# SwiGLU on one core: first loads in pairs from two queues, a block of x turned on TensorE, up of the first tiles on 512 columns

## The chip, the cores and the metric

One core of one Trainium2 chip. The metric is the device time of one execution in microseconds (us), as the median over several executions; profiles are of single executions on the same core. A profile's span is about 1.8 us shorter than the time of its execution (81.3 against 83.13 for the kernel before).

Words used below: DVE is the vector engine (VectorE); SP is the engine that issues most of the DMAs (`nc.sync`). A "gate" or an "up" is one matmul of the gate or up product; the "ups of the first tiles" are those of F tiles 0 to 3. A "D block" is 128 of the 512 values of D. A "turn" is a matmul with the identity that swaps rows and columns of a 128 x 128 piece of x; its result lies in PSUM and is copied to SBUF ("the copy"). A load has "landed" when all its bytes have arrived.

## The reference

```python
# x: (32, 32, 512); w1, w3: (512, 1792); w2: (1792, 512); all bfloat16
gate = einsum("bsd,df->bsf", x, w1)
up   = einsum("bsd,df->bsf", x, w3)
out  = einsum("bsf,fd->bsd", silu(gate) * up, w2)
```

With the first two axes of x flattened there are 1024 rows. Gate and up are computed transposed, F on partitions (14 tiles of 128) and rows along the free axis in two blocks of 512, each as 4 matmuls over the D blocks of 128.

## The kernel before

TensorE needs x with D on partitions. The first 256 rows are loaded plainly and turned on TensorE; rows 256 to 511 (the "second quarter" below) and the second block of 512 come by transposing DMAs. While the data arrive, the first four F tiles are worked on by halves of 256 columns.

```python
    nc.sync.dma_start(out=x_sb[:], in_=x_view[:, 0 : HB // P, :])            # HB = 256
    for w_sb, w_v in ((w1_sb, w1_v), (w3_sb, w3_v)):
        load_w(w_sb, w_v, 0, FK, 0, 2)       # tiles 0..3, D blocks 0 and 1; FK = 4
        load_w(w_sb, w_v, 0, FK, 2, DT)      # tiles 0..3, D blocks 2 and 3
    nc.sync.dma_start_transpose(out=xT[:, :, HB:NB], in_=x_flat[HB:NB, :])   # NB = 512
    # ... the other loads of w1 and w3, the second block of x, w2 (cut) ...

    keep_warm(6, NB)                          # matmuls of ones, to warm TensorE up
    keep_warm(2, P)
    transpose_slab(0, nc.vector.tensor_copy)  # two transposes into PSUM (bf16), one copy
    transpose_slab(1, nc.scalar.copy)
    keep_warm(3, P)
    gates = [bank("gate_ps") for _ in range(FK)]
    for dt in range(DT):                      # gates of tiles 0..3, first 256 columns
        for fo in range(FK):
            project(gates[fo], w1_sb, fo, 0, HB, [dt])
        if dt == 0:
            transpose_slab(2, nc.vector.tensor_copy)
            transpose_slab(3, nc.scalar.copy)
    ups = [bank("up_ps") for _ in range(FK)]
    for dt in range(DT):                      # ups of tiles 0..3, first 256 columns
        for fo in range(FK):
            project(ups[fo], w3_sb, fo, 0, HB, [dt])
    for fo in range(FK):                      # second 256 columns of both
        project(gates[fo], w1_sb, fo, HB, NB, range(DT), HB)
        project(ups[fo], w3_sb, fo, HB, NB, range(DT), HB)
        swiglu(gates[fo], ups[fo], fo, 0)     # ScalarE sigmoid, two DVE products
    # ... all other tiles on 512 columns, then the output matmuls (cut) ...
```

Of the kernel before, what the change touches and what calls it, by code (L numbers as in the profile page):

```python
# [9 lines left out]
@with_exitstack  # L10
def kernel(
    ctx: ExitStack,
    tc: tile.TileContext,
    x: bass.AP,
    w1: bass.AP,
    w3: bass.AP,
    w2: bass.AP,
    out: bass.AP,
):
    nc = tc.nc  # L20
    P = nc.NUM_PARTITIONS
    fp32 = mybir.dt.float32
    bf16 = mybir.dt.bfloat16
    SIGMOID = mybir.ActivationFunctionType.Sigmoid

    B, S, D = x.shape
    F = w1.shape[1]
    N = B * S
    NB = 512
    HB = NB // 2  # L30
    DT = D // P
    FT = F // P
    NT = N // P
    NBLK = N // NB
    assert D % P == 0 and F % P == 0 and N % NB == 0

    x_flat = x.flatten_outer_dims()
    out_flat = out.flatten_outer_dims()
    w1_v = w1.rearrange("(dt p) f -> p dt f", p=P)
    w3_v = w3.rearrange("(dt p) f -> p dt f", p=P)  # L40
    w2_v = w2.rearrange("(ft p) d -> p ft d", p=P)

    consts = ctx.enter_context(tc.tile_pool(name="consts", bufs=1))
    work = ctx.enter_context(tc.tile_pool(name="work", bufs=3))
    psum = ctx.enter_context(tc.tile_pool(name="psum", bufs=8, space=bass.MemoryType.PSUM))

    ctx.enter_context(tc.manual_schedule())

    x_view = x_flat.rearrange("(nt p) d -> p nt d", p=P)
    ident = consts.tile([P, P], bf16, name="ident")  # L50
    make_identity(nc, ident[:])
    x_sb = consts.tile([P, HB // P, D], bf16, name="x_sb")
    xT = consts.tile([P, DT, N], bf16, name="xT")
    w1_sb = consts.tile([P, DT, F], bf16, name="w1_sb")
    w3_sb = consts.tile([P, DT, F], bf16, name="w3_sb")
    w2_sb = consts.tile([P, FT, D], bf16, name="w2_sb")
    hT = consts.tile([P, FT, N], bf16, name="hT")

    FK = 4

    def load_w(w_sb, w_v, c0, c1, d0=0, d1=DT):
        f0, f1 = c0 * P, c1 * P
        nc.sync.dma_start(out=w_sb[:, d0:d1, f0:f1], in_=w_v[:, d0:d1, f0:f1])  # L63

    nc.sync.dma_start(out=x_sb[:], in_=x_view[:, 0 : HB // P, :])  # L65
    for w_sb, w_v in ((w1_sb, w1_v), (w3_sb, w3_v)):
        load_w(w_sb, w_v, 0, FK, 0, 2)
        load_w(w_sb, w_v, 0, FK, 2, DT)
    nc.sync.dma_start_transpose(out=xT[:, :, HB:NB], in_=x_flat[HB:NB, :])
    for c0, c1 in ((FK, 6), (6, 10), (10, FT)):  # L70
        load_w(w1_sb, w1_v, c0, c1)
        load_w(w3_sb, w3_v, c0, c1)
    nc.sync.dma_start_transpose(out=xT[:, :, NB:N], in_=x_flat[NB:N, :])
    FH = FT // 2
    nc.sync.dma_start(out=w2_sb[:, 0:FH, :], in_=w2_v[:, 0:FH, :])
    nc.sync.dma_start(out=w2_sb[:, FH:FT, :], in_=w2_v[:, FH:FT, :])

    one = nc.const_aps.tensor(1.0, [P, 1], bf16)
    table = consts.tile([P, 1], fp32, name="table")
    nc.scalar.activation(table[:], one, SIGMOID)  # L80

    def bank(name):
        return psum.tile([P, NB], fp32, name=name, tag="bank")

    warm_ps = bank("warm_ps")

    def keep_warm(n, cols):
        for _ in range(n):
            nc.tensor.matmul(  # L89
                warm_ps[:, 0:cols],  # L90
                lhsT=one.to_broadcast([P, P]),
                rhs=one.to_broadcast([P, cols]),
                start=True,
                stop=True,
            )

    def transpose_slab(dt, copy):
        pT = psum.tile([P, HB], bf16, name="pT", tag="bank")
        for nt in range(HB // P):
            nc.tensor.transpose(  # L100
                pT[:, nt * P : (nt + 1) * P], x_sb[:, nt, dt * P : (dt + 1) * P], ident[:]
            )
        copy(xT[:, dt, 0:HB], pT[:])  # L103

    def project(ps, w_sb, fo, n0, n1, dts, c0=0):
        for dt in dts:
            nc.tensor.matmul(  # L107
                ps[:, c0 : c0 + n1 - n0],
                lhsT=w_sb[:, dt, fo * P : (fo + 1) * P],
                rhs=xT[:, dt, n0:n1],  # L110
                start=(dt == 0),
                stop=(dt == DT - 1),
            )

    def swiglu(gate_ps, up_ps, fo, nb):
        sig = work.tile([P, NB], fp32, name="sig")
        nc.scalar.activation(sig[:], gate_ps[:], SIGMOID)  # L117
        t = work.tile([P, NB], fp32, name="t")
        nc.vector.tensor_mul(t[:], gate_ps[:], sig[:])  # L119
        nc.vector.tensor_mul(hT[:, fo, nb * NB : (nb + 1) * NB], t[:], up_ps[:])  # L120

    keep_warm(6, NB)
    keep_warm(2, P)
    transpose_slab(0, nc.vector.tensor_copy)
    transpose_slab(1, nc.scalar.copy)
    keep_warm(3, P)
    gates = [bank("gate_ps") for _ in range(FK)]
    for dt in range(DT):
        for fo in range(FK):
            project(gates[fo], w1_sb, fo, 0, HB, [dt])  # L130
        if dt == 0:
            transpose_slab(2, nc.vector.tensor_copy)
            transpose_slab(3, nc.scalar.copy)
    ups = [bank("up_ps") for _ in range(FK)]
    for dt in range(DT):
        for fo in range(FK):
            project(ups[fo], w3_sb, fo, 0, HB, [dt])
    for fo in range(FK):
        project(gates[fo], w1_sb, fo, HB, NB, range(DT), HB)
        project(ups[fo], w3_sb, fo, HB, NB, range(DT), HB)  # L140
        swiglu(gates[fo], ups[fo], fo, 0)

    for nb in range(NBLK):
        for fo in range(FK if nb == 0 else 0, FT):
            gate_ps = bank("gate_ps")
            project(gate_ps, w1_sb, fo, nb * NB, (nb + 1) * NB, range(DT))
            up_ps = bank("up_ps")
            project(up_ps, w3_sb, fo, nb * NB, (nb + 1) * NB, range(DT))
            swiglu(gate_ps, up_ps, fo, nb)

    for nt in range(NT):
        last = nt == NT - 1
        c0 = 0
        for DB in (D // 2, D // 4, D // 4) if last else (D,):
            o_ps = psum.tile([P, DB], fp32, name="o_ps", tag="bank")
            for fo in range(FT):
                nc.tensor.matmul(  # L157
                    o_ps[:],
                    lhsT=hT[:, fo, nt * P : (nt + 1) * P],
                    rhs=w2_sb[:, fo, c0 : c0 + DB],  # L160
                    start=(fo == 0),
                    stop=(fo == FT - 1),
                )
            o_sb = work.tile([P, DB], bf16, name="o_sb", tag="o_sb")
            if last:
                nc.vector.tensor_copy(o_sb[:], o_ps[:])  # L166
            else:
                nc.scalar.copy(o_sb[:], o_ps[:])  # L168
            nc.sync.dma_start(
                out=out_flat[nt * P : (nt + 1) * P, c0 : c0 + DB],  # L170
                in_=o_sb[:],
            )
            c0 += DB
# [30 lines left out]
```

## Time and profile before

| | kernel before |
|---|---|
| time, median of 3 (range) | 82.82 us (82.79 to 83.15) |
| span of the profile | 81.3 us |
| TensorE busy | 77.5 us, 95% |
| DVE / ScalarE busy | 48% / 28% |
| load that TensorE waits for last | w1, D blocks 2 and 3 of the first tiles: issued 1.75, landed 6.60 |
| last matmul starts | 78.40 us |

TensorE is one unbroken chain from 6.65 us to the end. The lines are in the prediction.

### The profile page before, as it was taken

Reading aid. Unit: us, or ns where it says so; the run is one execution under the profiler, and the core shown is the slowest. Engines: PE = TensorE matmul, PEld = TensorE weight load, DVE = VectorE, ACT = ScalarE, POOL = GpSimd, SP = SyncE. Lnnn points to the kernel's source line nnn. Section 1 sums busy time; section 2 is a strip of 40 time slices with the busy share of each in tenths; the row PEclk is TensorE's granted clock in tenths of the full one; section 3 lists DMA queues with packets and bytes.
Section 4 is the critical chain, followed back from the end, with each engine's and each line's share of the span. In section 5 each row is a group of like instructions: output and inputs, shape, how many; then the busy total and the mean of one; then the engine's idle time right before and its main releaser. Section 6 shows DMA issues by size and latency. Waiting matters only on the chain.

```text
span 81.3 us, 1079 instructions
## 1 busy us (share of the span) xinstructions
PE 77.5 (95%) x415; PEld 39.9 (49%) x415; DVE 39.3 (48%) x61; ACT 23.1 (28%) x39; POOL 0.7 (1%) x6
## 2 busy tenths in 40 slices
PE   6998999999999999999999999999999999999960
PEld 2486885444444444444444444444444444444850
DVE  0020078999987787887878887883000000000040
ACT  6020175322234322344222343220220211220200
POOL 3000000000000000000000000000000000000000
PEclk9999999999999999999999999999999999999998
DMA  0989999999996000000000000000011012011120
GB/s 10 293 265 166 281 333 350 355 85 222 300 349 221 1 0 0 0 0 0 8 4 0 0 0 0 0 0 0 9 56 64 24 49 69 25 40 64 37 76 16
DMA packets 10933, 7.67 MB, mean 94 GB/s; under 512 B 3760, under 2 KB 10928, under 8 KB 10928
## 3 DMA queue, kind: packets, MB, share of 16 engines
q1 hardware_dynamic: 10928, 7.60, 35.9%
q8 instruction: 3, 0.05, 0.3%
q14 instruction: 2, 0.02, 0.1%
HBM read 5.77 MB, written 1.05 MB: 84 GB/s over the span
## 4 chain that ended last, share of the span: by engine, by line
PE 88%; DMA 6%; SPq 1%; DVE 0%; issue 0%; DVEq 0%
PE o_ps L157 30%; PE up_ps L107 30%; PE gate_ps L107 29%; DMA w_sb<-in_w_dram 6%; SPq L63 1%; SPq L65 1%; DVE o_sb L166 0%; DVEq L166 0%
## 5 line engine op out<-in xcount | busy, mean ns | idle before, releaser
L107 PEld LDWEIGHTS <-w_sb 128*128 128x128 bf16 x256 | 25.1, 99 | 23.8 <-DMA w_sb<-in_w_dram 0.6
L107 PE MATMUL gate_ps<-xT,w_sb 128*128 128x512 bf16 (+1 forms) x128 | 29.7, 357 | 0.3 <-DMA w_sb<-in_w_dram 0.3
L107 PE MATMUL up_ps<-xT,w_sb 128*128 128x512 bf16 (+1 forms) x128 | 28.9, 352 | 0.0
L117 ACT ACTIVATE sig<-gate_ps 128x512 f32<-128x512 f32 x28 | 16.7, 598 | 31.1 <-PE gate_ps L107 30.0
L157 PE MATMUL o_ps<-w_sb,hT 128*128 128x512 bf16 (+2 forms) x140 | 24.4, 336 | 0.0
L119 DVE TENSOR_TENSOR t<-gate_ps,sig 128x512 f32<-128x512 f32 x28 | 19.3, 689 | 8.6 <-ACT sig L117 8.6
L120 DVE TENSOR_TENSOR hT<-t,up_ps 128x512 bf16<-128x512 f32 x28 | 19.3, 688 | 3.3 <-PE gate_ps L107 0.5
L157 PEld LDWEIGHTS <-hT 128*128 128x128 bf16 x140 | 12.6, 98 | 11.9
L166 DVE CAST o_sb<-o_ps 128x128 bf16<-128x128 f32 (+1 forms) x3 | 1.0, 336 | 22.3 <-PE o_ps L157 22.3
L168 ACT CAST o_sb<-o_ps 128x512 bf16<-128x512 f32 x7 | 4.1, 586 | 17.9 <-PE o_ps L157 17.9
L89 PE MATMUL warm_ps<-const-bfloat16-1.0 128*128 128x512 bf16 (+1 forms) x11 | 3.5, 483 | 0.8 <-PEq L188 0.8
L103 DVE COPY xT<-pT 128x256 bf16<-128x256 bf16 x2 | 0.6, 292 | 5.4 <-PE pT L100 5.4
L89 PEld LDWEIGHTS <-const-bfloat16-1.0 128*128 128x128 bf16 x11 | 1.4, 141 | 2.4 <-issue 2.4
L103 ACT COPY xT<-pT 128x256 bf16<-128x256 bf16 x2 | 0.7, 372 | 3.3 <-PE pT L100 3.3
L80 ACT ACT_TABLE_LOAD x1 | 1.3, 1283 | 0.7 <-PEq L188 0.7
L100 PE MATMUL pT<-ident,x_sb 128*128 128x128 bf16 x8 | 1.2, 308 | 0.0
L100 PEld LDWEIGHTS <-x_sb 128*128 128x128 bf16 x8 | 0.8, 138 | 0.3 <-DMA x_sb<-in_x_dram 0.2
masks.py:199 POOL TENSOR_SCALAR_AFFINE_SELECT ident<-ident 128x128 bf16<-128x128 bf16 x1 | 0.3, 294 | 0.1
masks.py:197 POOL MEMSET ident<- 128x128 bf16 x1 | 0.2, 205 | 0.3 <-POOLq L188 0.3
L80 ACT ACTIVATE table<-const-bfloat16-1.0 128x1 f32<-128x1 bf16 x1 | 0.2, 203 | 0.0
L188 POOL MEMSET const-bfloat16-1.0<- 128x1 bf16 x1 | 0.1, 102 | 0.0
L188 POOL MEMSET const-uint8-127<- 128x1 uint8 x1 | 0.1, 102 | 0.0
(2 smaller groups left out, 0.2 us busy)
## 6 DMA issues: line engine op xcount, KB each, us to landing
w_sb<-in_w_dram SPq DMA_DIRECT2D x4, 512.0 KB, 6.4
w_sb<-in_w_dram SPq DMA_DIRECT2D x2, 896.0 KB, 7.2
w_sb<-in_w_dram SPq DMA_DIRECT2D x6, 256.0 KB, 5.3
out_dram<-o_sb SPq DMA_DIRECT2D x7, 128.0 KB, 1.7
x_sb<-in_x_dram SPq DMA_DIRECT2D x1, 256.0 KB, 2.9
out_dram<-o_sb SPq DMA_DIRECT2D x1, 64.0 KB, 1.5
out_dram<-o_sb SPq DMA_DIRECT2D x2, 32.0 KB, 1.4
xT<-in_x_dram SPq DMA_TRANSPOSE x2, 8.1
```

What stands on the lines that cost most here:

```text
L63: nc.sync.dma_start(out=w_sb[:, d0:d1, f0:f1], in_=w_v[:, d0:d1, f0:f1])
L80: nc.scalar.activation(table[:], one, SIGMOID)
L89: nc.tensor.matmul(warm_ps[:, 0:cols], lhsT=one.to_broadcast([P, P]), rhs=one.to_broadcast([P, cols]), start=True, stop=True,)
L100: nc.tensor.transpose(pT[:, nt * P : (nt + 1) * P], x_sb[:, nt, dt * P : (dt + 1) * P], ident[:])
L103: copy(xT[:, dt, 0:HB], pT[:])
L107: nc.tensor.matmul(ps[:, c0 : c0 + n1 - n0], lhsT=w_sb[:, dt, fo * P : (fo + 1) * P], rhs=xT[:, dt, n0:n1], start=(dt == 0), stop=(dt == D ...
L117: nc.scalar.activation(sig[:], gate_ps[:], SIGMOID)
L119: nc.vector.tensor_mul(t[:], gate_ps[:], sig[:])
L120: nc.vector.tensor_mul(hT[:, fo, nb * NB : (nb + 1) * NB], t[:], up_ps[:])
L157: nc.tensor.matmul(o_ps[:], lhsT=hT[:, fo, nt * P : (nt + 1) * P], rhs=w2_sb[:, fo, c0 : c0 + DB], start=(fo == 0), stop=(fo == FT - 1),)
L166: nc.vector.tensor_copy(o_sb[:], o_ps[:])
L168: nc.scalar.copy(o_sb[:], o_ps[:])
```

## The change

Its intent: the first data should arrive sooner (two issuing queues instead of one), the transposing DMA of the second quarter should go from the opening (a plain load and eight turning matmuls in its place), and with all 512 columns of x on chip the up matmuls of the first tiles need not be cut in halves. PSUM, eight banks under one tag, becomes two tags of four banks each. The diff, its output part cut:

```diff
--- before.py
+++ after.py
@@ -42,14 +42,14 @@
 
     consts = ctx.enter_context(tc.tile_pool(name="consts", bufs=1))
     work = ctx.enter_context(tc.tile_pool(name="work", bufs=3))
-    psum = ctx.enter_context(tc.tile_pool(name="psum", bufs=8, space=bass.MemoryType.PSUM))
+    psum = ctx.enter_context(tc.tile_pool(name="psum", bufs=4, space=bass.MemoryType.PSUM))
 
     ctx.enter_context(tc.manual_schedule())
 
     x_view = x_flat.rearrange("(nt p) d -> p nt d", p=P)
     ident = consts.tile([P, P], bf16, name="ident")
     make_identity(nc, ident[:])
-    x_sb = consts.tile([P, HB // P, D], bf16, name="x_sb")
+    x_sb = consts.tile([P, NB // P, D], bf16, name="x_sb")
     xT = consts.tile([P, DT, N], bf16, name="xT")
     w1_sb = consts.tile([P, DT, F], bf16, name="w1_sb")
     w3_sb = consts.tile([P, DT, F], bf16, name="w3_sb")
@@ -58,18 +58,23 @@
 
     FK = 4
 
-    def load_w(w_sb, w_v, c0, c1, d0=0, d1=DT):
+    def load_x(queue, t0, t1):
+        queue.dma_start(out=x_sb[:, t0:t1, :], in_=x_view[:, t0:t1, :])
+
+    def load_w(queue, w_sb, w_v, c0, c1, d0=0, d1=DT):
         f0, f1 = c0 * P, c1 * P
-        nc.sync.dma_start(out=w_sb[:, d0:d1, f0:f1], in_=w_v[:, d0:d1, f0:f1])
-
-    nc.sync.dma_start(out=x_sb[:], in_=x_view[:, 0 : HB // P, :])
-    for w_sb, w_v in ((w1_sb, w1_v), (w3_sb, w3_v)):
-        load_w(w_sb, w_v, 0, FK, 0, 2)
-        load_w(w_sb, w_v, 0, FK, 2, DT)
-    nc.sync.dma_start_transpose(out=xT[:, :, HB:NB], in_=x_flat[HB:NB, :])
-    for c0, c1 in ((FK, 6), (6, 10), (10, FT)):
-        load_w(w1_sb, w1_v, c0, c1)
-        load_w(w3_sb, w3_v, c0, c1)
+        queue.dma_start(out=w_sb[:, d0:d1, f0:f1], in_=w_v[:, d0:d1, f0:f1])
+
+    load_x(nc.sync, 0, 1)
+    load_x(nc.scalar, 1, 2)
+    load_w(nc.sync, w1_sb, w1_v, 0, FK, 0, 2)
+    load_w(nc.scalar, w1_sb, w1_v, 0, FK, 2, DT)
+    load_x(nc.sync, 2, 4)
+    load_w(nc.scalar, w3_sb, w3_v, 0, FK, 0, 2)
+    load_w(nc.sync, w3_sb, w3_v, 0, FK, 2, DT)
+    for c0, c1 in ((FK, 8), (8, FT)):
+        load_w(nc.sync, w1_sb, w1_v, c0, c1)
+        load_w(nc.sync, w3_sb, w3_v, c0, c1)
     nc.sync.dma_start_transpose(out=xT[:, :, NB:N], in_=x_flat[NB:N, :])
     FH = FT // 2
     nc.sync.dma_start(out=w2_sb[:, 0:FH, :], in_=w2_v[:, 0:FH, :])
@@ -79,8 +84,8 @@
     table = consts.tile([P, 1], fp32, name="table")
     nc.scalar.activation(table[:], one, SIGMOID)
 
-    def bank(name):
-        return psum.tile([P, NB], fp32, name=name, tag="bank")
+    def bank(name, tag="any"):
+        return psum.tile([P, NB], fp32, name=name, tag=tag)
 
     warm_ps = bank("warm_ps")
 
@@ -94,13 +99,18 @@
                 stop=True,
             )
 
-    def transpose_slab(dt, copy):
-        pT = psum.tile([P, HB], bf16, name="pT", tag="bank")
-        for nt in range(HB // P):
-            nc.tensor.transpose(
-                pT[:, nt * P : (nt + 1) * P], x_sb[:, nt, dt * P : (dt + 1) * P], ident[:]
-            )
-        copy(xT[:, dt, 0:HB], pT[:])
+    def turn(half, dt, copy):
+        pT = bank("pT")
+        for k in range(HB // P):
+            nt = half * (HB // P) + k
+            nc.tensor.matmul(
+                pT[:, k * P : (k + 1) * P],
+                lhsT=x_sb[:, nt, dt * P : (dt + 1) * P],
+                rhs=ident[:],
+                start=True,
+                stop=True,
+            )
+        copy(xT[:, dt, half * HB : (half + 1) * HB], pT[:, 0:HB])
 
     def project(ps, w_sb, fo, n0, n1, dts, c0=0):
         for dt in dts:
@@ -119,30 +129,37 @@
         nc.vector.tensor_mul(t[:], gate_ps[:], sig[:])
         nc.vector.tensor_mul(hT[:, fo, nb * NB : (nb + 1) * NB], t[:], up_ps[:])
 
+    dve, act = nc.vector.tensor_copy, nc.scalar.copy
     keep_warm(6, NB)
-    keep_warm(2, P)
-    transpose_slab(0, nc.vector.tensor_copy)
-    transpose_slab(1, nc.scalar.copy)
+    turn(0, 0, dve)
+    turn(0, 1, act)
     keep_warm(3, P)
-    gates = [bank("gate_ps") for _ in range(FK)]
-    for dt in range(DT):
+    gates = [bank("gate_ps", "gate") for _ in range(FK)]
+
+    def gate_a(dt):
         for fo in range(FK):
             project(gates[fo], w1_sb, fo, 0, HB, [dt])
-        if dt == 0:
-            transpose_slab(2, nc.vector.tensor_copy)
-            transpose_slab(3, nc.scalar.copy)
-    ups = [bank("up_ps") for _ in range(FK)]
-    for dt in range(DT):
-        for fo in range(FK):
-            project(ups[fo], w3_sb, fo, 0, HB, [dt])
+
+    gate_a(0)
+    turn(0, 2, dve)
+    turn(0, 3, act)
+    gate_a(1)
+    gate_a(2)
+    turn(1, 0, dve)
+    turn(1, 1, act)
+    gate_a(3)
+    turn(1, 2, dve)
+    turn(1, 3, act)
     for fo in range(FK):
         project(gates[fo], w1_sb, fo, HB, NB, range(DT), HB)
-        project(ups[fo], w3_sb, fo, HB, NB, range(DT), HB)
-        swiglu(gates[fo], ups[fo], fo, 0)
+    for fo in range(FK):
+        up_ps = bank("up_ps")
+        project(up_ps, w3_sb, fo, 0, NB, range(DT))
+        swiglu(gates[fo], up_ps, fo, 0)
 
     for nb in range(NBLK):
         for fo in range(FK if nb == 0 else 0, FT):
-            gate_ps = bank("gate_ps")
+            gate_ps = bank("gate_ps", "gate")
             project(gate_ps, w1_sb, fo, nb * NB, (nb + 1) * NB, range(DT))
             up_ps = bank("up_ps")
             project(up_ps, w3_sb, fo, nb * NB, (nb + 1) * NB, range(DT))
 ... (the output tile takes tag "any" of the same pool)
```

## The prediction

> **What bounds the kernel now.** I read the page first (busy shares, the 40 slices, the chain that ended last), then the chain in order of time, then the timeline of the first 10 us, engine by engine, because every line of the change but the PSUM pools lies there.
>
> ```profile
> PE 77.5 (95%) x415; PEld 39.9 (49%) x415; DVE 39.3 (48%) x61; ACT 23.1 (28%) x39; POOL 0.7 (1%) x6
> PE   6998999999999999999999999999999999999960
> PE 88%; DMA 6%; SPq 1%; DVE 0%; issue 0%; DVEq 0%
> ```
>
> TensorE is the bound: one slice of 2 us in the opening is at 8 tenths, the rest at 9 until the tail, and 88% of the chain is matmuls. The only thing in front of them is one load, as the chain in time shows:
>
> ```profile
> 1.75 4.85 DMA w_sb<-in_w_dram
> 6.65 1.05 PE gate_ps L107 x8
> 54.37 24.26 PE o_ps L157 x140
> ```
>
> The load is the second half of w1's first four tiles (D blocks 2 and 3): issued at 1.75, landed at 6.60. From 6.65 to 78.6 TensorE never waits. So the end moves only by (a) how much useful matmul work is done before that point, (b) what work is added behind it, (c) any new stall. The timeline of PE before that point:
>
> ```profile
> 3.66 0.61 PE L100 MATMUL pT<-ident,x_sb 128*128 128x128 bf16 x4
> 4.06 0.52 PE L89 MATMUL warm_ps<-const-bfloat16-1.0 128*128 128x128 bf16 x3
> 4.43 1.01 PE L107 MATMUL gate_ps<-xT,w_sb 128*128 128x256 bf16 x4
> 5.24 0.63 PE L100 MATMUL pT<-ident,x_sb 128*128 128x128 bf16 x4
> 5.66 0.65 PE L107 MATMUL gate_ps<-xT,w_sb 128*128 128x256 bf16 x4
> 6.65 1.05 PE L107 MATMUL gate_ps<-xT,w_sb 128*128 128x256 bf16 x8 [0.33 <-DMA w_sb<-in_w_dram]
> ```
>
> Columns are start, length, group. Spacing comes from differences of starts: four gates of 256 columns take 5.24-4.43 = 0.81 us (203 ns each) at first, but eight from 6.65 to 7.53 take 110 ns each. TensorE doubles its rate at about 5.7 us (the matmuls at 5.66 are the first at the fast spacing). Warm, 512 columns cost 216 ns (four from 12.77 to 13.63). 128 columns cost 56 ns: the copies of the last two output tiles start at 77.93 and 78.71, with 14 such matmuls between. Cold, 128 columns cost 105 ns ((4.06-3.66)/4, roughly, and 106 at 5.24 to 5.66).
>
> The idle time that a better opening can recover: at 6.1 to 6.65, about 0.49 us (602 ns between two starts that are otherwise 110 apart), and the warm-up matmuls at 4.06, which fill a wait for w1. That is all.
>
> **What the Trainium skill says.** (1) "DMA: Bandwidth & Descriptors", section Issuing engines are not separate DMA queues: transfers started by different engines run on the same 16 DMA engines and interleave, so two issuers save only the issue time. The trace has an issue at 0.45 to 0.51 us and the DMA share at 0.98 in the stretches from 2.5 to 4.0, so the issuer is not what the data wait for. (2) The same page, Queues, rings and completion order: each DMA engine takes turns between the rings that have work. No run yet has two issuing queues, so the trace cannot say. (3) "TensorE: Matmul & The Clock Gate", Part 1: the array starts at half rate and is released after a busy window of about 3.4 us, free-running. The trace agrees in effect (203 then 110 ns); the column of granted clock has 1.00 there and does not show it. (4) "VectorE: DVE Perf Modes", Why PSUM operands drop a tier: an fp32 operand in PSUM is copied at the basic rate. The trace agrees:
>
> ```profile
> L103 DVE COPY xT<-pT 128x256 bf16<-128x256 bf16 x2 | 0.6, 292 | 5.4 <-PE pT L100 5.4
> L166 DVE CAST o_sb<-o_ps 128x256 bf16<-128x256 f32 x1 | 0.4, 425 | 21.5 <-PE o_ps L157 21.5
> ```
>
> **The change, part by part.**
>
> *Transposed load of x's second quarter removed, eight matmuls added.* The transposing DMA occupied DMA engines from about 6.2 to 8.3 (bytes fall to 78 to 191 GB/s there), but nobody waited for it: it landed at 9.20, when TensorE got there at 9.28. So its removal gives the end nothing. In its place: 8 matmuls x 56 ns = 0.45 us, in TensorE's program order ahead of gates, so on the path. Turning by plain matmul leaves fp32 in PSUM, so each DVE copy grows from 292 to 425 ns; that is on the path where a gate follows soon. From the last turning matmul's start to the first user: 219 ns (its length) + 40 (to the copy) + 425 + 45 = 0.73 us. Ahead of the second-half gates, D block 2 comes only two turning matmuls and two gates after (about 0.39 us), so 0.34 us of stall; ahead of the first-half gates on block 2, 0.605 us lies between, so 0.12 us if warm. ScalarE's copies (372 ns) have one gate more and just fit.
>
> *Up of the first tiles on 512 columns.* 32 x 109 = 3.49 us become 16 x 216 = 3.45 us: -0.04 us. It also starts later, which only matters if w3 were late; here w3 was there at 8.2 and is now needed at about 10.
>
> *Loads in pairs.* Bytes ahead of the last w1 half are the same 768 KB (x 256, w1 256 + 256). What changes is the order: w1's two halves, formerly one after the other, now share the engines. In the stretches of half a microsecond the DMA moved 231, 283, 340, 313, 203, 223, 270 GB/s from 2.0 on, which reaches 512 KB at about 3.8 and 768 KB near 5.0. Formerly the first half landed at 4.28. Interleaved, both halves finish with the 768 KB: the first half lands at about 5.1 (my estimate, 4.4 to 5.7: two rings may hide some latency and beat these rates), the second at 5.2 to 6.6.
>
> *PSUM in two pools of four.* In steady state DVE needs 2 x 0.69 = 1.38 us per pair and TensorE 1.73, so each tile is free long before its turn. Worth 0.
>
> Sum for TensorE, w1's first half at 5.1: gates on block 0 start 5.15, three at the cold 213 ns and one at 110, done 5.90; four turns 6.12; gates block 1 6.56; stall to 6.69; gates block 2 7.13; x's second quarter is the fourth 256 KB of six, about 1.0 to 1.3 MB, which the old trace moved by 6.6: with landing 6.9 to 7.5, say 0.1 of stall; four turns 7.45; gates block 3 7.89; four turns 8.11; 16 gates of the second half 1.75 + 0.34 of stall: 10.20. The old kernel is equally far after 24 matmuls from 6.65, at 9.27. Difference +0.93, less 0.04: **+0.9 us**. With w1's first half at 4.4 as before, the same sum has 4.45 to 5.3, then cold turns 5.7, blocks 1 and 2 6.6, turns 6.8, block 3 7.26, turns 7.48, second half 9.57: **+0.3 us**. At 5.6: **+1.1 us**. I weigh these 0.35, 0.4, 0.25, for +0.7, and shade it down to +0.6, since the opening was surely arranged by someone who hoped for early data: 82.82 + 0.6 = **83.4 us**.
>
> **The rivals.**
> 1. *The pairs work*: two rings hide the long packets of 4 to 5 us and all of w1 is there by 4.2. For it: the rate falls to 203 GB/s there, against 350 later. Even then TensorE runs cold until 5.7, and the 0.45 us of added matmuls and 0.34 us of copy wait eat the recovered 0.49: -0.3 to +0.2 us, 82.5 to 83.0. Over 2% is out of reach: x cannot land much before 3.4, and TensorE from there needs 72.0 + 0.87 (8 gates) + 0.9 (16 turns) us warm plus about 1.2 of cold loss, which ends at 78.4 against 78.6 now.
> 2. *TensorE stays cold longer*: the gap between 4.3 and 5.15 leaves the window only two thirds busy, and the release slips by a window of 3.4 us. Up to 1.7 us of rate lost: 84.5 to 85.2. Against it: TensorE has been busy since 0.8. About one in ten.
> 3. *x's second quarter lands late* (straggling DMA engines: the old fourth load took 5.1 us to land): block 3 waits behind the turns in program order, +0.5 us on top: 83.9 to 84.2.
>
> **Range and chances.** Low end 82.6 from rival 1, high end 84.4 from late w1 plus rival 3. Faster by 2% needs 81.2, below what rival 1 can give: 0.01. Slower by 2% needs 84.5: rival 2, or everything late: 0.09.
>
> **What would show it.** In the new profile: the chain should still begin with a DMA of w or x, then matmuls to the end. First gates near 5.15 and not 4.43; eight turns of the second quarter at 56 ns; a PE wait for a DVE copy of about 0.3 us ahead of the second-half gates; DVE copies at 425 ns; steady state and output stage unchanged in length. I am wrong if the first gates start by 4.5, if the copy waits are absent, if the fast spacing starts much earlier or later than 5.7, or if a stall appears after 10 us.

## The result, and the profile after

| | before | after |
|---|---|---|
| first comparison: median (range) | 82.88 (82.79 to 83.15), 4 runs | 84.67 (83.81 to 85.51), 4 runs |
| ratio of the fast runs, 95% interval | | 1.0121 (1.0073 to 1.0169) |
| second comparison, 5 rounds: median (range) | 82.93 (82.64 to 83.15), 11 runs | 84.01 (83.55 to 84.31), 6 runs |
| ratio of the fast runs, 95% interval | | 1.0124 (1.0093 to 1.0155) |

A ratio here is the mean time of one kernel's fast runs over that of the other's of the same rounds, so not quite the ratio of the medians. The change makes the kernel 1.2% slower, 1.0 us: 82.82 x 1.0121 = 83.8. (Both intervals lie wholly above 1.) Two of its first four runs, 85.3 and 85.5, are slow (over 1.5% above the fastest) and not in the ratio; what they are is taken up below.

The page of the changed kernel, the lines that answer to those of before (TensorE busy, its 40 slices, shares of the chain):

```profile
PE 77.8 (95%) x405; PEld 38.1 (46%) x405; DVE 40.8 (50%) x63; ACT 23.5 (29%) x41; POOL 0.7 (1%) x6
...
PE   6988999999999999999999999999999999999960
...
PE 87%; DMA 7%; SPq 1%; DVE 1%; issue 0%; DVEq 0%
```

Nothing but the opening differs: a second slice at 8 tenths. The chain in order of time (start, length, what) says which load it now begins with, and that a DVE copy has come into it:

```profile
1.65 5.50 DMA x_sb<-in_x_dram
...
7.20 0.40 PE pT L106 x4
7.60 0.44 PE gate_ps L117 x4
8.04 0.13 PE pT L106 x2
...
8.19 0.44 DVE xT L113
...
8.66 1.69 PE gate_ps L117 x14
10.35 3.45 PE up_ps L117 x16
```

The end hangs no longer on w1's second half but on x's second quarter, which lands at 7.16 and not 6.60. The timeline of TensorE up to the point where both kernels have finished the gates of the first four tiles:

```profile
3.43 0.67 PE L106 MATMUL pT<-ident,x_sb 128*128 128x128 bf16 x4
3.89 0.53 PE L94 MATMUL warm_ps<-const-bfloat16-1.0 128*128 128x128 bf16 x3
4.81 0.86 PE L117 MATMUL gate_ps<-xT,w_sb 128*128 128x256 bf16 x4 [0.39 <-DMA w_sb<-in_w_dram]
5.50 0.39 PE L106 MATMUL pT<-ident,x_sb 128*128 128x128 bf16 x4
5.73 1.16 PE L117 MATMUL gate_ps<-xT,w_sb 128*128 128x256 bf16 x8
7.20 0.40 PE L106 MATMUL pT<-ident,x_sb 128*128 128x128 bf16 x4 [0.31 <-DMA x_sb<-in_x_dram]
7.44 0.60 PE L117 MATMUL gate_ps<-xT,w_sb 128*128 128x256 bf16 x4
7.87 0.39 PE L106 MATMUL pT<-ident,x_sb 128*128 128x128 bf16 x4
8.10 0.38 PE L117 MATMUL gate_ps<-xT,w_sb 128*128 128x256 bf16 x2
8.66 1.69 PE L117 MATMUL gate_ps<-xT,w_sb 128*128 128x256 bf16 x14 [0.19 <-DVE xT L113]
```

Read the starts. Four turns take 5.73 - 5.50 = 0.23 us, 56 ns each. Between 5.73 and 7.20 eight gates (0.87 us, and 0.13 of a first copy wait) are followed by 0.48 us of waiting for x. Between 8.10 and 8.66 lie two gates (0.22) and 0.35 us of waiting for the copy. The brackets show less than that, since the modelled length of a matmul (219 to 273 ns) is longer than its spacing. The up matmuls start at 10.19; the kernel before is equally far at 9.27. The copies are the fp32 ones:

```profile
L113 DVE CAST xT<-pT 128x256 bf16<-128x256 f32 x4 | 1.7, 424 | 6.9 <-PE pT L106 6.9
```

The account of the two traces, in starts of the last matmul: 79.27 - 78.40 = 0.87 us. Of this, 0.56 is the later landing (7.16 - 6.60), and 0.31 is what lies behind it: 79.27 - 7.16 = 72.11 us in the changed kernel against 78.40 - 6.60 = 71.80. The 0.31 are eight turns (0.45) and the copy wait (0.35), less four gates of block 2 that are now done ahead of the load (0.44), less the saving of the wider up matmuls (0.04): 0.32.

The 0.31 comes back in every full-rate trace of this order of work; the 0.56 is of one pair of traces alone. A second trace of the changed kernel (below) has the landing at 6.68, only 0.08 later, and the one trace of the kernel before is of a run at the upper end of its range (83.13). An estimate of the usual shift comes from the times: in all traces the time exceeds the start of the last matmul by 4.73 to 4.82 us, so the fast runs' means of 82.9 and 83.9 stand for landings near 6.3 and 7.0, if the same load decides in each run. That is 0.7 us later, and 0.7 + 0.31 is the loss of 1.0.

### The profile page after: what moved, and what is told of

Its sections match the earlier page's. It is cut to its first block, busy times and chain, and to the rows that moved or that the text cites.

```text
span 82.2 us, 1062 instructions
## 1 busy us (share of the span) xinstructions
PE 77.8 (95%) x405; PEld 38.1 (46%) x405; DVE 40.8 (50%) x63; ACT 23.5 (29%) x41; POOL 0.7 (1%) x6
## 2 busy tenths in 40 slices
DMA packets 9109, 7.67 MB, mean 93 GB/s; under 512 B 2704, under 2 KB 9104, under 8 KB 9104
## 4 chain that ended last, share of the span: by engine, by line
PE 87%; DMA 7%; SPq 1%; DVE 1%; issue 0%; DVEq 0%
PE o_ps L174 29%; PE up_ps L117 29%; PE gate_ps L117 28%; DMA x_sb<-in_x_dram 7%; PE pT L106 1%; DVE xT L113 1%; SPq L66 1%; SPq L62 0%; DVE o_sb L183 0%; DVEq L183 0%
## 5 line engine op out<-in xcount | busy, mean ns | idle before, releaser
L117 PEld LDWEIGHTS <-w_sb 128*128 128x128 bf16 x240 | 23.4, 98 | 25.8 <-DMA w_sb<-in_w_dram 0.7
L117 PE MATMUL up_ps<-xT,w_sb 128*128 128x512 bf16 x112 | 28.2, 379 | 0.0
L113 DVE CAST xT<-pT 128x256 bf16<-128x256 f32 x4 | 1.7, 424 | 6.9 <-PE pT L106 6.9
L113 ACT CAST xT<-pT 128x256 bf16<-128x256 f32 x4 | 1.5, 372 | 3.5 <-PE pT L106 3.5
L106 PE MATMUL pT<-ident,x_sb 128*128 128x128 bf16 x16 | 1.8, 240 | 0.3 <-DMA x_sb<-in_x_dram 0.3
```

The lines of the kernel that those rows point to most:

```text
L106: nc.tensor.matmul(pT[:, k * P : (k + 1) * P], lhsT=x_sb[:, nt, dt * P : (dt + 1) * P], rhs=ident[:], start=True, stop=True,)
L113: copy(xT[:, dt, half * HB : (half + 1) * HB], pT[:, 0:HB])
L117: nc.tensor.matmul(ps[:, c0 : c0 + n1 - n0], lhsT=w_sb[:, dt, fo * P : (fo + 1) * P], rhs=xT[:, dt, n0:n1], start=(dt == 0), stop=(dt == D ...
```

## The experiments

My theory A was that account. Rivals: the pairs of queues alone do the harm; the copy wait or the turns lie in idle time and cost nothing; and, for the high runs, theory B (TensorE is released late to its full rate) against theory C (late landings). Twelve runs were made of ten kernels, all correct, on three chips; the kernel before ran beside each batch (11 times each: medians 82.93, 83.00, 82.87). Across chips only the ratios to it are compared.

### The changed kernel again

No edit.

> The changed kernel once more, unaltered, beside the kernel before: two of its four runs so far took 85.3 and 85.5 us, two 83.8 and 84.0. Theory A (the loss is in the opening: 0.45 us of added turning matmuls, 0.35 of copy wait, 0.48 of waiting for x's second quarter, less the waits that went away): fast runs about 0.9 us above before, 83.7 to 84.0. Theory B (TensorE's release to full rate slips in some runs because of the gap at 4.2 to 4.8 us): again two groups of runs, the upper one 1.3 to 1.7 us above the lower. If the runs all fall in one group, the two high runs were a disturbance.

Measured: 84.01 us (83.55 to 84.31), ratio 1.0124 (1.0093 to 1.0155). The 1.2% stand. No high run this time, so the two of the first four are not in every set of runs. In its trace x's second quarter landed at 6.68 and the last matmul started at 78.79: again 72.11 between them.

### The pairs alone

```diff
-    nc.sync.dma_start(out=x_sb[:], in_=x_view[:, 0 : HB // P, :])
-    for w_sb, w_v in ((w1_sb, w1_v), (w3_sb, w3_v)):
-        load_w(w_sb, w_v, 0, FK, 0, 2)
-        load_w(w_sb, w_v, 0, FK, 2, DT)
+    nc.sync.dma_start(out=x_sb[:, 0:1, :], in_=x_view[:, 0:1, :])
+    nc.scalar.dma_start(out=x_sb[:, 1:2, :], in_=x_view[:, 1:2, :])
+    load_w(w1_sb, w1_v, 0, FK, 0, 2)
+    load_w(w1_sb, w1_v, 0, FK, 2, DT, nc.scalar)
+    load_w(w3_sb, w3_v, 0, FK, 0, 2, nc.scalar)
+    load_w(w3_sb, w3_v, 0, FK, 2, DT)
```

> The kernel before with only its first loads issued in pairs from SP and ScalarE; x's second quarter still comes by the transposing DMA and up still on 256 columns. Theory A: w1's second half lands about 5.9 instead of 6.6 and its first half about 4.8 instead of 4.3, so the wait at 6.1 goes and the chain gains about 0.45 us: 82.3 to 82.5, a ratio of 0.994 to 0.996. Rival (pairs are what costs, by delaying w1's first half by 0.5 us): 83.1 to 83.4.

Measured: 83.71 us (83.19 to 85.14, the last slow), ratio 1.0091 (1.0054 to 1.0129). My expectation was wrong; the pairs by themselves cost 0.75 us. TensorE's timeline in this form:

```profile
5.04 1.03 PE L109 MATMUL gate_ps<-xT,w_sb 128*128 128x256 bf16 x4 [0.59 <-DMA w_sb<-in_w_dram]
5.87 0.47 PE L102 MATMUL pT<-ident,x_sb 128*128 128x128 bf16 x4
6.18 1.47 PE L109 MATMUL gate_ps<-xT,w_sb 128*128 128x256 bf16 x12
8.09 1.16 PE L109 MATMUL up_ps<-xT,w_sb 128*128 128x256 bf16 x9 [0.43 <-DMA w_sb<-in_w_dram]
```

The wait at 6.1 is indeed gone (twelve gates in a row), as expected. But the first gates start at 5.04 and not 4.43, and the up matmuls wait to 8.09 for w3's first half, which landed at 8.04; in the kernel before it had landed at 7.36, in time for the ups at 7.53. So in pairs the load needed earlier finishes later, twice over. The two halves of w1 landed 0.2 to 1.1 us apart in the nine traces with pairs and 1.9 to 2.3 us apart on one queue: they share the engines, as the prediction said. In the changed kernel w3's first half is as late (8.18), but there its ups come only at 10.19: the later ups hide what the pairs do to w3.

### The pairs alone, w3's halves exchanged

```diff
-    load_w(w3_sb, w3_v, 0, FK, 0, 2, nc.scalar)
-    load_w(w3_sb, w3_v, 0, FK, 2, DT)
+    load_w(w3_sb, w3_v, 0, FK, 0, 2)
+    load_w(w3_sb, w3_v, 0, FK, 2, DT, nc.scalar)
```

> The kernel before with its first loads in pairs, as in the second run of this study, but with the two halves of w3 exchanged between the queues: the half needed first from SP, the other from ScalarE. There the third load of ScalarE landed at 8.04 and the third of SP at 7.36, and up waited for the former by 0.6 us. Theory A (the loss of the pairs alone is that wait): the wait goes, 0.6 us faster than that form, 82.9 to 83.2, about the same as before. Rival (the late first gates at 5.04 are the loss): still 83.5 or more.

Measured: 83.26 us (83.20 to 83.43), ratio 1.0062 (1.0027 to 1.0097). Between the expectation and its rival. The load the ups need landed at 7.53 and they started at 7.58, still after a wait:

```profile
7.58 1.59 PE L109 MATMUL up_ps<-xT,w_sb 128*128 128x256 bf16 x13 [0.68 <-DMA w_sb<-in_w_dram]
```

From that landing to the last matmul there are 70.93 us in both forms (8.04 to 78.97; 7.53 to 78.46). So the end hangs on w3's first half in both, and the exchange gains what it lands earlier, 0.5 us in the traces; by the ratios, on two chips, it is 0.24 us, with intervals of about 0.3 us either side. In these two traces with pairs it lands at best 0.17 us later than in the kernel before. The remaining 0.6% is larger than the traces show (last matmul at 78.46 against 78.40); the one trace of the kernel before is of a slow one of its fast runs, so that part stays open.

### The rest of the change on one queue

```diff
-    load_x(nc.sync, 0, 1)
-    load_x(nc.scalar, 1, 2)
+    load_x(nc.sync, 0, 2)
     load_w(nc.sync, w1_sb, w1_v, 0, FK, 0, 2)
-    load_w(nc.scalar, w1_sb, w1_v, 0, FK, 2, DT)
+    load_w(nc.sync, w1_sb, w1_v, 0, FK, 2, DT)
     load_x(nc.sync, 2, 4)
-    load_w(nc.scalar, w3_sb, w3_v, 0, FK, 0, 2)
+    load_w(nc.sync, w3_sb, w3_v, 0, FK, 0, 2)
```

> The changed kernel with all its first loads issued from SP alone, in the order x first quarter, w1 halves, x second quarter, w3 halves. Theory A: first gates at about 4.4, blocks 2 at 6.6, then a wait for x's second quarter to 7.2 or 7.4, so the end is within 0.2 us of the changed kernel: the pairs hardly matter to it. Rival (the pairs are the cause of the loss): 0.5 us or more faster than the changed kernel.

Measured: 83.96 us (83.70 to 84.21), ratio 1.0123 (1.0100 to 1.0147), the same as the changed kernel beside it (1.0124). In its timeline:

```profile
4.37 0.60 PE L116 MATMUL gate_ps<-xT,w_sb 128*128 128x256 bf16 x4 [0.23 <-DVE xT L112]
...
6.36 0.61 PE L116 MATMUL gate_ps<-xT,w_sb 128*128 128x256 bf16 x4 [0.72 <-DMA w_sb<-in_w_dram]
7.09 0.40 PE L105 MATMUL pT<-ident,x_sb 128*128 128x128 bf16 x4
...
8.54 0.70 PE L116 MATMUL gate_ps<-xT,w_sb 128*128 128x256 bf16 x5 [0.18 <-DVE xT L112]
```

The first gates are earlier (4.37) and the gates of block 2 later (6.36) than with pairs, and none of it matters: x's second quarter landed at 7.04, and 72.11 us later the last matmul started. TensorE was even at its full rate by 4.4 us in this execution (four gates in 0.44 us), to no avail, since it only waits the longer. So the rest of the change (plain load, turns, wider ups, PSUM) costs the whole 1.2% with or without pairs, and the pairs' own 0.9% is not added, because the end hangs on one landing, not on a sum.

### Removing the copy wait

The second-half gates block by block, so that eight gates lie between the last turns and the first use of their copies. First on the changed kernel:

```diff
-    for fo in range(FK):
-        project(gates[fo], w1_sb, fo, HB, NB, range(DT), HB)
+    for dt in range(DT):
+        for fo in range(FK):
+            project(gates[fo], w1_sb, fo, HB, NB, [dt], HB)
```

> The changed kernel with the second-half gates in the order block by block over the four tiles, so eight gates of 109 ns lie between the last turns and the first use of what they give. Theory A: the PE wait for the DVE copy (458 ns between two starts, 0.35 over the usual 109) goes, and the end comes 0.35 us earlier: fast runs 83.4 to 83.6. Rival (the wait is hidden by a later wait, for w3 or for the last w1 load): no change.

Measured: 84.74 us (83.89 to 85.53), ratio 1.0197 (1.0148 to 1.0247), unclear: 84.19, 85.53, 85.14, 84.36, 83.89, 85.12. A miss by the clock, although in its trace the wait is gone and only 71.77 us lie between x's landing (7.67) and the last matmul. Two of its high runs counted as fast in that ratio (85.14 and 85.12 are just under 1.5% above 83.89), so it isn't evidence on the wait. The single-queue form with the same edit gave tighter runs:

> The single-queue form of the changed kernel with the second-half gates block by block over the four tiles. The single-queue form has tight runs (83.70 to 84.21), unlike the two forms with pairs, so a difference of 0.3 us can be read here. Theory A (the wait for the DVE copy is 0.35 us of the path): 83.5 to 83.7 us, a ratio to before of 1.008. Rival (removing it does nothing, as the median of the form with pairs seemed to say): 83.9 to 84.0.

Measured: 83.65 us (83.43 to 84.82, the last slow), ratio 1.0067 (1.0033 to 1.0100), as against 1.0123 without the edit. The timeline has no wait ahead of the sixteen gates:

```profile
7.57 0.39 PE L105 MATMUL pT<-ident,x_sb 128*128 128x128 bf16 x4
7.80 1.91 PE L116 MATMUL gate_ps<-xT,w_sb 128*128 128x256 bf16 x16
```

71.76 us lie between x's landing (6.86) and the last matmul, 0.35 less. The ratios differ by 0.0056, 0.46 us, more than the 0.35 of the traces but on another chip, with intervals of 0.003 either side. The copy wait is on the path; the rival is out.

### Doubling the turns

```diff
-        for k in range(HB // P):
+        for k in [k for k in range(HB // P) for _ in range(1 + half)]:
```

> The single-queue form with every turning matmul of x's second quarter issued twice in a row (same result, eight more matmuls of 128 columns, whose warm spacing is 56 ns). Theory A (the turns lie on TensorE's path behind the landing of x's second quarter): 0.45 us slower than the single-queue form, 84.3 to 84.5. Rival (the turns lie in idle time and cost nothing): 83.9 to 84.1.

Measured: 84.52 us (84.10 to 85.08), ratio 1.0179 (1.0135 to 1.0224; unclear as to the 2%), 0.46 us above the single-queue form by the ratios. The timeline:

```profile
7.25 0.62 PE L105 MATMUL pT<-ident,x_sb 128*128 128x128 bf16 x8
7.71 0.60 PE L116 MATMUL gate_ps<-xT,w_sb 128*128 128x256 bf16 x4
```

Eight turns in 0.46 us, where four took 0.23. From x's landing (7.20) to the last matmul are 72.51 us, 0.40 more than 72.11: the missing 0.05 came off the copy wait, since more turns lie ahead of the gate that waits. Turns are on the path at 56 ns each.

### The kernel before with the critical load cut in two

```diff
-    for w_sb, w_v in ((w1_sb, w1_v), (w3_sb, w3_v)):
-        load_w(w_sb, w_v, 0, FK, 0, 2)
-        load_w(w_sb, w_v, 0, FK, 2, DT)
+    load_w(w1_sb, w1_v, 0, FK, 0, 2)
+    load_w(w1_sb, w1_v, 0, FK, 2, 3)
+    load_w(w1_sb, w1_v, 0, FK, 3, DT)
+    load_w(w3_sb, w3_v, 0, FK, 0, 2)
+    load_w(w3_sb, w3_v, 0, FK, 2, DT)
```

> The kernel before with the second half of w1's first tiles loaded in two DMAs of one D block each, nothing else. Theory A (the end of the kernel before hangs on the landing of that load at 6.6, which its slowest DMA engines set): block 2 lands by about 5.6 to 6.1, the wait of 0.49 us at 6.1 shrinks, and the kernel is 0.2 to 0.45 us faster than before, ratio 0.995 to 0.998, unless block 3 or w3, now 0.05 to 0.1 us later, stop it instead. Rival (a straggling engine delays any load of that moment, however it is cut): same as before, 82.8 to 83.0.

Measured: 83.06 us (82.46 to 83.51), ratio 1.0004 (0.9960 to 1.0048). No gain shown. In the traced run (82.84) D block 2 landed at 6.00, as hoped, and the last matmul started at 78.02, 0.38 us earlier than before, although the ups now waited to 7.12 for w3. But its runs scatter over 1 us, the mean is that of before, and the trace of before that it is set against is of a slow one of its fast runs (83.13). What held the slower of them was not traced; it stays open.

### What the high runs are

> One more look at the form with pairs and block-by-block second half, in the hope of a trace of one of its high runs (three of six lay at 85.1 to 85.5). In all traces so far of kernels with the turns, the last matmul starts 72.11 us (71.77 without the copy wait) after the landing of x's second quarter. Theory C (high runs are late landings from the two queues): in a high run that load lands about 1.2 us later, near 8.5, and the 71.77 hold. Theory B (late release to full rate): the landing is at 7 to 7.7 and 256-column gates stay at 213 ns beyond 6 us.

This single look (state unknown) took 85.77 us, span 84.0: a high run. TensorE's timeline:

```profile
3.28 0.63 PE L106 MATMUL pT<-ident,x_sb 128*128 128x128 bf16 x4
3.71 0.53 PE L94 MATMUL warm_ps<-const-bfloat16-1.0 128*128 128x128 bf16 x3
5.56 1.04 PE L117 MATMUL gate_ps<-xT,w_sb 128*128 128x256 bf16 x4 [1.33 <-DMA w_sb<-in_w_dram]
6.39 0.64 PE L106 MATMUL pT<-ident,x_sb 128*128 128x128 bf16 x4
6.82 1.92 PE L117 MATMUL gate_ps<-xT,w_sb 128*128 128x256 bf16 x8
8.53 0.63 PE L106 MATMUL pT<-ident,x_sb 128*128 128x128 bf16 x4
8.95 1.06 PE L117 MATMUL gate_ps<-xT,w_sb 128*128 128x256 bf16 x4
9.80 0.54 PE L106 MATMUL pT<-ident,x_sb 128*128 128x128 bf16 x4
```

Eight gates from 6.82 to 8.53 take 0.21 us each, twice the 0.109 of the fast runs; four gates at 8.95 take 0.21 each still. The fast spacing is there only from about 10.1 us. x's second quarter landed at 6.93, earlier than in the changed kernel's own trace. So this run is theory B, not C: w1's first half landed at 5.52, TensorE stood idle for 1.33 us by the bracket (1.5 by the spacing: 1.64 between two starts, less 0.11) up to 5.56, and the release to the full rate slipped from the 3.4 to 6.1 us of the other traces to 10.1. From x's landing to the last matmul (81.01) are 74.08 us, 2.3 more than the 71.77 of this form at the full rate.

The packed traces also hold the times at which the full clock was granted (the page prints 1.00 before the first grant as well). In this run it is 10.12 us; in the eleven others that have such a record it is 3.44 to 5.76. The stretch at full clock that follows lasts 75.09 us here and in the kernel before and 78.51 in the ten others, a difference of 3.4 us. And the length of an idle stretch alone does not decide: in the first trace of this form TensorE stood idle from 4.22 to 5.18, 1.0 us, and the grant came at 4.71, in the midst of it.

If the idle stretch causes the slip, filling it should end the high runs. On the form with the block-by-block second half, with a control, and on the changed kernel:

```diff
-    keep_warm(3, P)
+    keep_warm(12, P)
```

> Control on this chip: the form with pairs and the block-by-block second half, unaltered. It has had four high runs in seven, and the trace of one showed full rate only from 10.1 us, after an idle stretch of TensorE from 3.9 to 5.56. Expected of theory B: again some runs near 83.6 to 84.4 and some 1.0 to 1.5 us higher.

> The same with twelve instead of three 128-column warm-up matmuls between the first turns and the first gates: 9 x 107 ns more at the cold rate, so TensorE is busy to about 5.2 us. Theory B (the idle stretch lets the release to full rate slip by a window): no run above 84.5, at no cost in the fast runs, since they wait for x's second quarter to about 7 anyway: 83.4 to 84.0. Theory C (late landings): the high runs stay, as many as in the control.

> The changed kernel itself with twelve instead of three warm-up matmuls there. Theory B: all runs between 83.5 and 84.3, none of the 85.3 and 85.5 seen in two of its first four; mean about 0.9 to 1.0 us above before. Theory C: high runs as before.

| form | runs, sorted | over 84.6 |
|---|---|---|
| control | 83.36 83.39 83.89 84.37 84.66 84.95 | 2 of 6 |
| control, 12 warm-up matmuls | 83.81 83.85 83.89 83.91 84.19 84.23 | 0 of 6 |
| changed kernel, 12 warm-up matmuls | 83.84 84.00 84.15 84.27 84.43 84.58 | 0 of 6 |

Over all batches the changed kernel and the control form without the longer warm-up had 8 runs of 23 above 84.6 (2 of 10 and 6 of 13), with it none of 12. If the 8 high runs lay by chance among all 35, none would be in these 12 with a chance of 2%; on the last chip alone, with its 2 high runs in 18, of 10%. The line at 84.6 was drawn afterwards; the expectation named 84.5, and one run (84.58) is above it. The one trace and the cure agree, so I take B as supported, not as shown for every high run: only one was traced. Two high runs lie outside this count: one of the pairs alone (85.14) and one of the single-queue form without the copy wait (84.82), in whose own trace TensorE has no such idle stretch. One expectation was missed: the six runs of the changed kernel with twelve warm-up matmuls were to lie between 83.5 and 84.3 with a mean of 0.9 to 1.0 us above before; two lie above, and the mean is 1.4 us above. The fast runs did not get faster, as they wait for x anyway; by ratio they are no better (1.0143 for the control form, against 1.0115 without; 1.0171, unclear as to the 2%, for the changed kernel, against 1.0124 on another chip). Even over all six runs the control form's mean hardly moves, 84.10 without and 83.98 with: the longer warm-up narrows the scatter. In the two traces x's second quarter landed at 7.72 and 6.99, and 71.77 and 72.11 us followed, as in every trace at the full rate. Whether the longer warm-up itself costs 0.2 us, by shifting where the loads land, stays open.

No form was shown to beat the kernel before. The best with the turns, the single-queue form without the copy wait, is 0.7% slower. Not tried: the four gates of block 3 need nothing of x's second quarter, whose turns stand ahead of them in program order, and their share of w1 had landed at 5.85. Put ahead of those turns they would fill up to 0.44 us of the 0.48 us of waiting (an estimate from the trace of the changed kernel).

## Why the prediction was right

It gave 83.4 us, range 82.6 to 84.4, within 2%; the ratio makes it 83.8. (The median of its first four runs, two of them high, is 84.67, above the range.) The mechanism, work added behind the load that TensorE waits for last, was right; the sum named the wrong landing as the one that matters. By its own steps:

- **TensorE's chain from the last awaited load to the end.** Right. But the sum's three cases, +0.3, +0.9 and +1.1, differ only in when w1's first half lands, and that does not decide: on one queue it landed at 4.25 and its gates started at 4.37, for which the sum says +0.3, and the kernel was as slow as with pairs (1.0123 against 1.0124). What decides is the landing of x's second quarter. In the traces whose rate is full, landing plus a constant gives the last matmul:

| kernel | load that decides | landed | last matmul starts | between |
|---|---|---|---|---|
| before | w1, blocks 2 and 3 | 6.60 | 78.40 | 71.80 |
| changed | x, second quarter | 7.16 | 79.27 | 72.11 |
| changed, again | same | 6.68 | 78.79 | 72.11 |
| one queue | same | 7.04 | 79.15 | 72.11 |
| one queue, no copy wait | same | 6.86 | 78.62 | 71.76 |
| one queue, turns doubled | same | 7.20 | 79.71 | 72.51 |
| pairs alone | w3, first half | 8.04 | 78.97 | 70.93 |

- **Added turns, 0.45 us on the path.** Right: 56 ns each in the trace, and doubling them cost 0.40 by the trace, 0.46 by the ratios.
- **Copy wait, 0.34 us, and 0.12 at block 2.** Right: 0.35 and 0.13, and taking the former away gained 0.35 by the traces.
- **Removing the transposing DMA is worth nothing, 512 columns 0.04 us, PSUM pools nothing.** Right as far as the traces show: no other wait of TensorE appears after 8.66. None of the three was run alone.
- **The pairs delay w1's first half.** Right in kind: it landed at 4.76 in the profile where I had 5.1, and at 4.66 to 5.52 over the other traces with pairs.
- **x's second quarter.** The landing was estimated at 6.9 to 7.5 and came at 7.16, but I charged 0.1 us of stall where 0.48 was measured. The gates ahead of it were done 0.4 us earlier than I had them, so the same end, ups at 10.19 against my 10.20, came by way of a longer wait. The two errors cancel because the end hangs on the landing; that the sum's end came out to 0.01 us was luck.
- **The weight.** My case of +0.9 is what the pair of traces shows. The case with the largest weight, +0.3, contradicts the sum's own estimate: it has the second quarter's turns start at 6.6, before the 6.9 to 7.5 at which x was to land. It pulled 83.7 down, and the shading to +0.6 for the author's hopes, with no line of the profile behind it, did the rest; so 83.4 is further off than the mechanism was.
- **Late release to the full rate, "about one in ten".** Named with the right mechanism, but under-weighted (8 of 23 runs of the forms with pairs and turns are high, 2 of 10 of the changed kernel itself) and under-sized (up to 1.7 us, where the traced run lost 2.3).

In the experiments I was wrong once on a matter of substance: I expected the pairs alone to gain 0.45 us, from looking only at the load that the kernel before waits for and not at the next one. The load cut in two, which I expected to gain 0.2 to 0.45 us, gained nothing by the clock either.

## What to carry to other kernels

When TensorE is one chain from the opening on, find the load it waits for last and count the work behind that landing. Work moved ahead of it is saved, until another load becomes the last; work added behind it costs in full (eight more turns of 56 ns cost 0.40 to 0.46 us here). In these kernels two queues made the load that is needed first land later (w1's first half at 4.66 to 5.52 us, against 4.17 to 4.28), so look at order of need before splitting loads between queues. And keep TensorE busy until it has reached its full rate: in the one high run that was traced, an idle stretch of 1.5 us in the opening went with a full rate 4 us later than in any other trace.

## What the Trainium skill lacked or had wrong

- "DMA: Bandwidth & Descriptors", Issuing engines are not separate DMA queues: it says that two issuers share the DMA engines and save only the issue time; the runs agree (the pairs alone were 0.9% slower, not faster). It does not say what sharing does to the load needed first: w1's first half landed at 4.66 to 5.52 us with pairs, at 4.17 to 4.28 on one queue.
- "TensorE: Matmul & The Clock Gate", Why this matters for your kernels: it asks for at least 4 us of unbroken work to reach the full rate, and warns of idle gaps over about 3 us. In the high run a gap of 1.5 us after 3.3 us of unbroken work went with a release at 10.1 us; in another run of that form the release came at 4.7 us, inside a gap of 1.0 us. How full the time before a release must be is not said. Part 1 puts the spread of the transition at 0.5 us either way; here it came at 5.76 us in the kernel before and at 3.55 in the same kernel with one load cut in two, and between 3.4 and 6.1 us in all traces but that of the high run.
- The same page, Part 4: PE-mode transpose: it gives about 275 ns for a transpose in a kernel. At the full rate the transposes of the kernel before have a length of 219 ns and a spacing of 56 ns (trace of its form with the load cut in two), and so have the plain matmuls that take their place in the changed kernel. The spacing is what they cost on the path, as the doubling of the latter confirmed.
- No page gives the scatter of landings of the same load: x's second quarter landed between 6.68 and 7.72 us in the ten traces that load it plainly (seven with pairs, three on one queue), which is as large as the whole effect under study.
